# One spread of the reciprocals instead of eight, its product placed later, and rests of weights kept further from their roundings

## The chip, the core and the metric

The kernel runs on one core of a Trainium2 chip. The core has five engines that run side by side and wait for each other by semaphores: TensorE (PE, with its weight loads PEld), VectorE (DVE), ScalarE (ACT), GpSimd (POOL) and SyncE (SP). SP, POOL and ACT also issue DMAs, which sixteen DMA engines carry out. The metric is the device time of one execution in microseconds; lower is better. A profile is one execution recorded by the hardware profiler.

## The reference: what is computed

One input `x` of 2048 rows and 512 columns goes through two branches, and a gate mixes them. The attention branch has 32 heads of width 16 that share one set of keys and values. The other branch is a dense layer of width 1792 with a squared ReLU.

```python
g = _sigmoid((x * gate_w).sum(-1, keepdims=True))
# attention: 32 query heads of width 16, one key and one value head
scores = jnp.einsum("bhqd,bkd->bhqk", q, k) * (Dh ** -0.5)
p = _softmax(scores, axis=-1)
o = jnp.einsum("bhqk,bkd->bhqd", p, v)
a = o.transpose(0, 2, 1, 3).reshape(B, S, H * Dh) @ wo
# dense branch
r = jnp.where(h > 0, h, 0)          # h = x @ w1 + b1
b = (r * r) @ w2 + b2
return g * a + (1 - g) * b
```

## The kernel before

**Tiles and loops.** The 2048 queries are cut into 4 chunks of 512 (`NC`, `CH`), the 32 heads into 8 groups of 4 (`NG`). For each chunk and group the kernel walks over the 16 tiles of 128 keys and over the two halves of the chunk: 1024 steps in all. A step computes scores of 128 keys for 4 heads and 256 queries on PE, their exponentials on ACT (`e`), and then the context products on PE (`acc<-e,v_ext`). The values carry a column of ones, so that `acc` holds the sums of the exponentials beside the unnormalised outputs. Everything in single precision that needs full accuracy is split into a rounded part and a rest (`w1r` and `w1l`, for example), and each product is made from three terms.

**Phases.** The program is written out by a planner in Python at build time. It emits PE's work in phases of 6 or 7 steps: scores, mixed with the products of the dense branch, of the query projection or of the output projection ("units", L1144), by fixed patterns (`PLANS`), and behind them the context products of a phase (L825). Most scores go to PSUM tiles `s`, which ACT reads directly (L802). Some go to a single PSUM bank `x`; DVE copies them to `e` (L786, "copy"), and only then may PE write `x` again.

**What sets DVE's order.** The planner keeps estimated times of PE, ACT and DVE (`at_pe`, `at_act`, `at_dve`). Work for DVE that isn't bound to a place stands in lists: rests of weights, `divisions`, and `chores` (casts and rests of other tiles). Ahead of each copy `spend()` places as much of it as fits until that copy's scores are due. An entry of `divisions` has a duration and a time from which it may run; a rest of weights may run from the estimated end of its rounding plus `SURE`, if ACT did the rounding. None of these numbers is a wait in the program: they only decide where in DVE's queue an instruction stands. What it waits for there, semaphores decide.

**A division.** When a pair of head groups is finished (15 times in the main path), ACT copies `acc` to `accs`, SP moves the outputs to `oc` and the sums to `lq`. DVE clamps the sums and notes whether that changed them, and takes reciprocals (`n`, L854). They lie 32 to a partition, and must be repeated for the 16 rows of each head. So POOL writes `n` to HBM (`ls<-n`, L855) and reads it back spread over 128 partitions (`lc<-ls`, L857). DVE then multiplies (`oc<-oc,lc`, L864), and POOL writes the result to HBM (`oTs<-oc`, L898), from where SP loads it back into `stage` for the output projection (L1000, for the last pair L1017).

**POOL's other work.** POOL's queue is in order. It also holds the stores of the queries' rests (`qs<-ql`, L358) in the first 160 us, the fills of `res` with the bias (L697, four for each chunk), and the loads and stores of the projection (`big<-ress` L217, `out<-big` L221).

**A unit's roundings.** When a hidden unit of the dense branch is done, DVE adds the bias and clamps (L675), squares (L676), rounds (`hr`, L195) and takes the rest (L196).

Of the kernel before, what the change touches and what calls it, by code (L numbers as in the profile page):

```python
# [15 lines left out]
OP = mybir.AluOpType  # L16
# [6 lines left out]
NC, CH = 4, 512  # L23
# [9 lines left out]
ROOT = float(0x1fbd1df5 + 0x80000)  # L33
WARM = 10
LW = 4 * CH // 64
LANDS, DIVIDES, WRITES, SPREADS, SURE = 6.0, 10.0, 14.0, 8.0, 0.7
PAIR, CONTEXT, TURN, EXP, COPY, LATE = 0.235, 0.429, 0.36, 0.925, 0.66, 0.3
GROUPS = (0, 1, 2, 3), (4, 5, 6, 7), (8, 9, 10), (11, 12, 13)
AHEAD = 4
# [19 lines left out]
LAST_OK = NC * KT - 1  # L59
# [106 lines left out]
def mix_kernel(ctx: ExitStack, tc: tile.TileContext, xT, wkv, wq, wo, w12, b1, b2, cst, out):  # L166
    nc = tc.nc
# [7 lines left out]
    ls = dram.tile([NC * KT, 8, CH], F32, name="ls")  # L175
# [55 lines left out]
    with fast, tc.tile_pool(name="at", bufs=1) as at, \  # L231
# [616 lines left out]
        def divide(o, l, i, ready):  # L848

            n = at.tile([128, LW], F32, name="n")  # L850
            wide = at.tile([128, CH], F32, name="lc", bufs=2)

            def over():
                nc.vector.reciprocal(n, n)  # L854
                nc.gpsimd.dma_start(ls[i].rearrange("a (b n) -> (a b) n", b=16), n)  # L855
                for k in range(8):
                    nc.gpsimd.dma_start(wide[16 * k:16 * k + 16], bass.AP(tensor=ls.tensor, offset=ls[i, k].offset,  # L857
                                                                          ap=[[0, 16], [1, CH]]))

            return ((0.1, ready, lambda: nc.vector.tensor_scalar(n, l, L_MIN, L_MAX, op0=OP.max, op1=OP.min)),  # L860
                    (0.2, ready, lambda: nc.vector.scalar_tensor_tensor(l, n, 1.0, l, op0=OP.mult, op1=OP.is_equal,
                                                                        accum_out=ok[:, i:i + 1])),
                    (0.3, ready, over),
                    (0.72, ready + SPREADS, lambda: nc.vector.tensor_tensor(o, o, wide, OP.mult)))  # L864

        sums = []

        def finish(it, q, acc):
# [25 lines left out]
            if u == 1:  # L894
                divisions.extend(divide(o, l, 4 * c + t, at_act + (LANDS if (c, t) == (NC - 1, 2) else DIVIDES)))

                def done():
                    nc.gpsimd.dma_start(oTs[it - 1:it + 1].rearrange("u d n -> (u d) n"), o)  # L898
                    complete.add((c, t))

                divisions.append((0.0, 0.0, done))
# [443 lines left out]
```

## Time and profile before

| | us |
|---|---|
| three runs | 1226.89, 1227.65, 1228.5 (median 1227.65) |
| profiled execution | 1226.17 |
| its span | 1224.4 |
| busy: PE / ACT / DVE / POOL | 1194.5 / 1058.2 / 743.2 / 131.4 |
| DVE's 524 copies `e<-x` | 362.4, with 396.4 idle before them |
| ACT's exponentials, from PSUM / from copies | 748.5 / 278.1 |
| POOL's 120 issues of the spread `lc<-ls` | 58.2 |
| granted clock of TensorE, mean | 0.994 of full speed |

A row of the timeline gives start, length, engine, line of the program, operation, output and inputs, and in brackets the idle time of that engine before it with what ended it. Idle time of an engine matters only where another one waits for it in turn. The views of waits give the sum, the number of times and the longest.

### The profile page before, as it was taken

To read this page: it belongs to the slowest core of one execution; us is meant where nothing else is said; L and a number is where in the kernel's file an instruction comes from. 1 tells how busy PE (TensorE), PEld (TensorE's weight loads), DVE (VectorE), ACT (ScalarE), POOL (GpSimd) and SP (SyncE) were. 2 spreads that over 40 slices of the span, in tenths; PEclk is the share of its full clock that TensorE was granted. 3 is DMA by queue.
4 is the path that set the end of the run, shared out by engine and by line. 5 is a ranking of instruction groups with operands and counts; after the bars stand their busy time and mean duration, and the time that the engine had idled before them with its cause. 6 is when DMAs were issued, how large, how long until landed. Compare 5 with 4: busy or idle time off the path is not lost.

```text
span 1224.4 us, 31785 instructions
## 1 busy us (share of the span) xinstructions
PE 1194.5 (98%) x13686; PEld 788.2 (64%) x13686; DVE 743.2 (61%) x1221; ACT 1058.2 (86%) x1211; POOL 131.4 (11%) x222
## 2 busy tenths in 40 slices
PE   9999899999999999999999999999999999999997
PEld 4566566666666666665666666666666666666663
DVE  6766476666655755646647755657448655566333
ACT  6798699888999989888998988899998898889883
POOL 1001211001010110101003021100104011010100
PEclk9999899999999999999999999999999999999999
DMA  6334332121222223101313123201222222111101
GB/s 227 86 101 120 96 100 66 48 68 54 66 88 92 80 63 105 58 28 50 96 53 114 62 64 104 63 28 53 72 80 71 88 64 95 36 46 34 39 36 37
DMA packets 49338, 89.71 MB, mean 73 GB/s; under 512 B 14362, under 2 KB 14858, under 8 KB 48680
## 3 DMA queue, kind: packets, MB, share of 16 engines
q1 hardware_dynamic: 36664, 64.58, 17.0%
q0 software_dynamic: 12384, 22.77, 6.3%
q8 instruction: 109, 1.79, 0.6%
q14 instruction: 37, 0.30, 0.1%
q10 hardware_dynamic: 144, 0.26, 0.1%
HBM read 61.76 MB, written 21.22 MB: 68 GB/s over the span
## 4 chain that ended last, share of the span: by engine, by line
PE 43%; issue 42%; POOL 5%; DMA 5%; DVE 3%; ACT 1%; DVEq 0%; POOLq 0%; SPq 0%; ACTq 0%
PE acc L825 17%; PE mm L1144 14%; PE s L765 9%; POOL lc L857 3%; DMA ls<-n 3%; PE x L765 2%; DMA lc<-ls 1%; DVE e L786 1%; POOL res L697 1%; DMA xf<-in_xT 0%; POOL out L221 0%; PE mm L299 0%; DVE oc L864 0%; ACT e L802 0%; PE mm L203 0%
## 5 line engine op out<-in xcount | busy, mean ns | idle before, releaser
L802 ACT ACTIVATE e<-s 128x1024 f32<-128x1024 f32 x762 | 748.5, 1029 | 120.7 <-PE s L765 61.6
L786 DVE COPY e<-x 128x512 f32<-128x512 f32 x524 | 362.4, 692 | 396.4 <-PE x L765 308.8
L825 PE MATMUL acc<-e,v_ext 128*32 128x256 f32 (+1 forms) x8064 | 475.8, 385 | 0.0
L765 PE MATMUL s<-qa,k_aug 49*128 49x512 f32 x1524 | 440.7, 416 | 0.1
L825 PEld LDWEIGHTS acc<-e,v_ext 128*32 128x32 f32 x8064 | 246.4, 110 | 198.6 <-issue 54.7
L765 PEld LDWEIGHTS s<-qa,k_aug 49*128 49x128 f32 x1524 | 230.7, 185 | 97.0 <-ACT e L802 73.4
L802 ACT ACTIVATE e<-e 128x1024 f32<-128x1024 f32 x262 | 278.1, 1062 | 12.7 <-DVE e L786 12.6
L765 PE MATMUL x<-qa,k_aug 49*128 49x512 f32 x524 | 220.2, 420 | 19.4 <-DVE e L786 17.2
L1144 PE MATMUL mm<-w2r,hr 64*128 64x512 f32 x752 | 157.7, 393 | 0.0
L765 PEld LDWEIGHTS x<-qa,k_aug 49*128 49x128 f32 x524 | 96.6, 184 | 49.7 <-DVE e L786 27.9
L1144 PEld LDWEIGHTS mm<-w2r,hr 64*128 64x128 f32 x752 | 105.5, 187 | 12.8 <-issue 0.8
L1144 PE MATMUL mm<-w2l,hr 64*128 64x512 f32 x376 | 91.9, 392 | 0.0
L855 POOL DMA_DIRECT2D ls<-n x15 | 8.4, 562 | 587.0 <-DVE n L854 524.9
L1144 PE MATMUL mm<-xlagain,w1r 64*128 64x512 f32 x224 | 66.9, 392 | 0.0
L1144 PE MATMUL mm<-xragain,w1r 64*128 64x512 f32 x224 | 66.4, 392 | 0.0
L1144 PE MATMUL mm<-xl,w1r 64*128 64x512 f32 x224 | 65.1, 391 | 0.0
L1144 PE MATMUL mm<-xr,w1r 64*128 64x512 f32 x224 | 65.1, 392 | 0.0
L1144 PEld LDWEIGHTS mm<-w2l,hr 64*128 64x128 f32 x376 | 58.3, 186 | 6.0
L857 POOL DMA_DIRECT2D lc<-ls x120 | 58.2, 492 | 32.8 <-DMA ls<-n 32.5
L1144 PE MATMUL mm<-more 64*128 64x512 f32 x216 | 58.1, 392 | 0.0
L1144 PE MATMUL mm<-xragain,w1l 64*128 64x512 f32 x224 | 51.1, 392 | 0.0
L1144 PE MATMUL mm<-xr,w1l 64*128 64x512 f32 x224 | 50.5, 392 | 0.0
(169 smaller groups left out, 1223.8 us busy)
## 6 DMA issues: line engine op xcount, KB each, us to landing
stage<-in_w SPq DMA_DIRECT2D x56, 256.0 KB
qa<-qs SPq DMA_DIRECT2D x186, 64.0 KB
w1f<-in_w SPq DMA_DIRECT2D x28, 256.0 KB
w2f<-in_w SPq DMA_DIRECT2D x28, 256.0 KB
qs<-qr SPq DMA_DIRECT2D x16, 256.0 KB
ress<-res POOLq DMA_DIRECT2D x4, 1024.0 KB, 4.3
qs<-ql POOLq DMA_DIRECT2D x15, 256.0 KB, 7.7
oc<-accs SPq DMA_DIRECT2D x30, 128.0 KB
```

What stands on the lines that cost most here:

```text
L697: nc.gpsimd.tensor_scalar(part, b2t[0], omg[:, s:s + 1], None, op0=OP.mult)
L765: nc.tensor.matmul(dst.rearrange("p (a n) -> p a n", a=2), k_aug[rows, kt * 128:(kt + 1) * 128], qa[it][rows, :, q * HC:q * HC + HC], star ...
L786: nc.vector.tensor_copy(e_half(u)[:, 2 * r:2 * r + 2], x.rearrange("p (a n) -> p a n", a=2))
L802: nc.scalar.activation(e_half(u), src, AF.Exp, scale=SCALE)
L825: nc.tensor.matmul(accs[q][h * 32:(h + 1) * 32], v_ext[:, kt], es[u // 2][:, h % 2 * 2 + h // 2, u % 2 * HC:u % 2 * HC + HC * n], start=(k ...
L855: nc.gpsimd.dma_start(ls[i].rearrange("a (b n) -> (a b) n", b=16), n)
L857: nc.gpsimd.dma_start(wide[16 * k:16 * k + 16], bass.AP(tensor=ls.tensor, offset=ls[i, k].offset, ap=[[0, 16], [1, CH]]))
L1144: nc.tensor.matmul((self.before if r else self).bank, a[p], b[p], start=not r and i == 0, stop=r == 1 and i == len(self.terms[1]) - 1, ski ...
```

## The change

`SPREADS`, the planner's distance from the estimated time of the reciprocals to the product, goes from 8 to 14, for the last division of the main path to 10. `SURE`, its distance from the end of a rounding on ACT to the rest of the same weights, goes from 0.7 to 1.4. The eight transfers that spread the reciprocals, each one row of 512 numbers repeated into 16 partitions, become one of eight rows, each repeated 16 times, into 128 partitions. Lines behind L857 have a number one lower in the changed kernel.

```diff
-LANDS, DIVIDES, WRITES, SPREADS, SURE = 6.0, 10.0, 14.0, 8.0, 0.7
+LANDS, DIVIDES, WRITES, SPREADS, SURE = 6.0, 10.0, 14.0, 14.0, 1.4
...
             def over():
                 nc.vector.reciprocal(n, n)
                 nc.gpsimd.dma_start(ls[i].rearrange("a (b n) -> (a b) n", b=16), n)
-                for k in range(8):
-                    nc.gpsimd.dma_start(wide[16 * k:16 * k + 16], bass.AP(tensor=ls.tensor, offset=ls[i, k].offset,
-                                                                          ap=[[0, 16], [1, CH]]))
+                nc.gpsimd.dma_start(wide, bass.AP(tensor=ls.tensor, offset=ls[i].offset,
+                                                  ap=[[CH, 8], [0, 16], [1, CH]]))
...
-                    (0.72, ready + SPREADS, lambda: nc.vector.tensor_tensor(o, o, wide, OP.mult)))
+                    (0.72, ready + (SPREADS if i < LAST_OK - 1 else LANDS + 4.0), lambda: nc.vector.tensor_tensor(o, o, wide, OP.mult)))
```

Since the numbers steer the planner, instructions move along the whole program. Two places show it.

DVE in the third division, from the reciprocals to the unit behind it, before:

```order
L854 RECIPROCAL n<-n 128x32
L786 COPY e<-x 128x2x256 x2
L700 SCALAR_TENSOR_TENSOR res_2278<-mm,omg,res_2278 128x512
L786 COPY e<-x 128x2x256 x2
L864 TENSOR_TENSOR oc<-oc,lc 128x512
L786 COPY e<-x 128x2x256 x2
L700 SCALAR_TENSOR_TENSOR res_2278<-mm,omg,res_2278 128x512
L786 COPY e<-x 128x2x256
L495 TENSOR_TENSOR w2l<-w2f,w2r 128x512
L786 COPY e<-x 128x2x256 x3
L675 TENSOR_SCALAR big<-mm,b1t 128x512
```

and in the changed kernel:

```order
L854 RECIPROCAL n<-n 128x32
L786 COPY e<-x 128x2x256 x2
L700 SCALAR_TENSOR_TENSOR res_2271<-mm,omg,res_2271 128x512
L786 COPY e<-x 128x2x256 x4
L700 SCALAR_TENSOR_TENSOR res_2271<-mm,omg,res_2271 128x512
L786 COPY e<-x 128x2x256
L863 TENSOR_TENSOR oc<-oc,lc 128x512
L786 COPY e<-x 128x2x256
L495 TENSOR_TENSOR w2l<-w2f,w2r 128x512
L786 COPY e<-x 128x2x256 x2
L675 TENSOR_SCALAR big<-mm,b1t 128x512
```

The product stands behind seven copies instead of four, and the rest `w2l` behind one copy more of its phase.

POOL in the fifth division, from the write of the reciprocals to the projection's first loads, before:

```order
L855 DMA ls<-n 128x32
L857 DMA lc<-ls 16x512 x8
L697 TENSOR_SCALAR res_5247<-big,omg 128x512
L898 DMA oTs<-oc 128x512
L697 TENSOR_SCALAR res_5247<-big,omg 128x512 x2
L217 DMA big<-ress 128x512 x2
```

and in the changed kernel:

```order
L855 DMA ls<-n 128x32
L856 DMA lc<-ls 128x1x512
L697 TENSOR_SCALAR res_5219<-big,omg 128x512 x2
L897 DMA oTs<-oc 128x512
L697 TENSOR_SCALAR res_5219<-big,omg 128x512
L217 DMA big<-ress 128x512 x2
```

Eight issues become one, and two of the fills of `res` stand between the spread and `oTs`, where one stood.

## The prediction

> **What bounds the kernel now.** I read the page first, then the chain that ended last in order of time, then busy time by stretches, then the waits, and last the timeline around one division.
>
> ```profile
> span 1224.4 us, 31785 instructions
> PE 1194.5 (98%) x13686; PEld 788.2 (64%) x13686; DVE 743.2 (61%) x1221; ACT 1058.2 (86%) x1211; POOL 131.4 (11%) x222
> ```
>
> PE is busy 98% of the span, so it looks as if only less work on PE could help. The ends of matmuls are modelled, though, so I look for PE's rhythm instead: where each block of context products (`acc`) starts.
>
> ```profile
> 286.65 3.16 PE acc L825 x56
> ...
> 294.42 3.16 PE acc L825 x56
> 302.22 3.16 PE acc L825 x56
> ...
> 951.36 3.16 PE acc L825 x56
> ...
> 1160.65 2.73 PE acc L825 x48
> 1167.34 2.73 PE acc L825 x48
> ```
>
> I call the time from one `acc` block to the next a phase. A phase of 56 context products takes 7.80 us (294.42 to 302.22), one of 48 takes 6.69 (1160.65 to 1167.34). The phases are so regular that whatever lengthens one can be read off directly. I cut out the phases in which DVE's product `oc*lc` of a division stands, with the phase behind the seventh: 16 stretches for 15 divisions, bounded by the starts of `acc`. Shown are the first, the last, those used below, and the sum over all 16 (columns: stretch, its length, PE's busy time and instructions, granted clock, DMA share, GB/s).
>
> ```profile
> 128.85:143.85 15.00, 10.79 (x97) 0.77 0.38 99
> ...
> 278.03:286.58 8.55, 8.02 (x96) 1.00 0.13 35
> ...
> 421.87:430.83 8.96, 7.25 (x73) 1.00 0.25 61
> ...
> 564.46:575.67 11.21, 8.48 (x95) 0.97 0.18 50
> 575.67:584.78 9.11, 9.11 (x96) 0.85 0.18 59
> ...
> 713.62:720.28 6.66, 6.66 (x73) 1.00 0.20 41
> ...
> 932.49:941.54 9.05, 8.07 (x96) 1.00 0.46 119
> ...
> 1147.23:1153.90 6.67, 6.67 (x80) 1.00 0.13 34
> sum 142.71, PE 127.05; mean PE 7.94
> ```
>
> Eleven of the 16 are phases of 56, three are phases of 48, and two are shorter ones with 32 context products; of these I take the one at 713.62 (6.66 us) as undisturbed. Without a disturbance they would take 11 x 7.80 + 3 x 6.69 + 2 x 6.66 = 119.2 us. They take 142.71: **23.5 us are lost there**, 7.2 of them in the first. The phases behind are 7.77 and 7.80 long (286.65, 294.42, 302.22), so nothing of a loss is caught up later. The clock column (0.77 in the first, 0.85 behind the seventh) shows that the loss holds a slower TensorE too.
>
> What causes it:
>
> ```profile
> DVE oc L864 <- DMA lc<-ls: 25.9, 13, 6.5
> ...
> PE x L765 <- DVE e L786: 17.2, 14, 3.7
> ```
>
> Thirteen times DVE stands still for `lc`, 25.9 us in all. In one division, from the timeline:
>
> ```profile
> 276.38 0.35 DVE L854 RECIPROCAL n<-n 128x32 f32<-128x32 f32 x1
> ...
> 277.05 0.55 POOL L855 DMA_DIRECT2D ls<-n  x1 [62.15 <-DVE n L854]
> ...
> 279.02 3.85 POOL L857 DMA_DIRECT2D lc<-ls  x8 [1.42 <-DMA ls<-n]
> ...
> 284.81 0.69 DVE L864 TENSOR_TENSOR oc<-oc,lc 128x512 f32<-128x512 f32 x1 [1.01 <-DMA lc<-ls]
> ...
> 286.16 0.49 PE L765 MATMUL x<-qa,k_aug 49*128 49x512 f32 x1 [0.53 <-DVE e L786]
> ```
>
> The reciprocals start at 276.38, the spread is issued from 279.02 (2.64 later) to 282.87, and the product starts at 284.81. Behind it on DVE is a copy of scores out of the single bank `x`, and PE's next scores for that bank wait for the copy.
>
> **The change part by part.**
>
> *One spread for eight.* POOL issues for 3.85 us now; the rows of single 128-partition transfers on POOL are 0.54 to 0.70. How long the new transfer takes to land is not in the trace. The nearest row is the load of `big`, 256 KB from HBM into 128 partitions on the same queue; the far end is the write of `ql`, 256 KB too, but split 4x32:
>
> ```profile
> L217 POOL DMA_DIRECT2D big<-ress x12: 536/543/611, 432.7 to 1017.0; - x12
> ...
> DMA to landing us min/median/max: 2.9/3.3/4.7
> ```
> ```profile
> L358 POOL DMA_DIRECT2D qs<-ql x15: 688/697/896, 38.2 to 155.4; - x15
> ...
> DMA to landing us min/median/max: 6.4/7.7/9.6
> ```
>
> I take 3.3; the ends are 2.9 and 9.6. `lc` is then whole 2.64 + 3.3 = 5.9 us after the reciprocals start, at worst 12.2.
>
> The Trainium skill, "DMA: Bandwidth & Descriptors", section "Why a DMA increments its semaphore by 16 and not by 1", speaks against this part: a transfer runs on the largest number of engines, up to 16, that divides the slowest dimension of both sides. By it the new spread (8x16 rows into 128 partitions) has 8 engines where each old one had 16, and its sum would put some 0.9 us on the landing and nothing on the time. The slow rows of `ql` (slowest dimension 4) agree with it.
>
> *The product further behind.* By the order it stands 4 to 9 copies of scores behind the reciprocals, before 2 to 4. The shortest distance that I find is in the fifth division, where it comes behind the sixth copy, the addition into `res` and a rounding:
>
> ```profile
> 419.47 0.35 DVE L854 RECIPROCAL n<-n 128x32 f32<-128x32 f32 x1
> ...
> 423.65 0.43 DVE L195 CAST hr<-big 128x512 fp32r<-128x512 f32 x1
> ...
> 430.87 0.69 DVE L786 COPY e<-x 128x512 f32<-128x512 f32 x1 [0.59 <-PE x L765]
> 431.48 0.74 DVE L700 SCALAR_TENSOR_TENSOR res<-mm,omg,res 128x512 f32<-128x512 f32 x1
> ```
>
> 431.48 + 0.74 + some 0.4 for the rounding, less the 2.23 that DVE waits there today, is 430.4: 10.9 us after the reciprocals. Elsewhere it is 11.3 to 15.7 by the same count. Against 5.9 that leaves 5 us; against the far end of 12.2 a few divisions would wait up to 1.3 us each, little beside today's 25.9. So the waits go, and with them **-23.5 us**. What is late next at those places is nothing that I find: a product of 0.69 then stands between two copies like a rest of weights, and phases with a rest take 7.80.
>
> The first division is special: its `ls` lands late, behind a write of `ql`.
>
> ```profile
> 129.15 3.87 POOL L857 DMA_DIRECT2D lc<-ls  x8 [7.57 <-DMA ls<-n]
> ```
>
> `lc` would be whole at 132.5 (with 3.3) to 138.8 (with 9.6); the product's place, three copies and one unit's roundings later, comes at some 134.6. I put **+0.5** (0 to 4) back.
>
> What is queued behind the product moves with it: POOL's write `oTs` (in the first division now behind a write of `ql`, in the fifth behind one more addition for `res`, in the ninth behind one load of `big`), and SP's reload of it, which the order also puts later, behind the stores of `accs`. No engine waits for these. The projection of the third chunk misses its turn and stands 9 phases later; the number of products in each phase stays the same up to the last eight phases, so PE has no gap there: 0.
>
> *The rests of weights.* Most of the 112 move one copy later, in the same phase. DVE's groups, first and last of five:
>
> ```profile
> L495 DVE TENSOR_TENSOR w1l<-w1f,w1r 128x512 fp32r<-128x512 f32 x28 | 19.1, 683 | 0.0
> ...
> L495 DVE TENSOR_TENSOR more<-stage,more 128x512 fp32r<-128x512 f32 x9 | 6.1, 681 | 0.0
> ```
>
> No rest waits for its rounding today (idle 0.0), so nothing can be gained. Lost could be PE time if a copy comes late; today rests stand behind the first, second or third copy of a phase, and phases of all three kinds take 7.8 us. I take 0; the ends are 0 and 11 (0.1 us for each).
>
> *POOL against DVE.* While POOL fills `res`, DVE's work from SBUF to SBUF runs longer:
>
> ```profile
> 941.38 6.35 POOL L697 TENSOR_SCALAR res<-big,omg 128x512 f32<-128x512 f32 x4
> ...
> 944.19 2.12 DVE L195 CAST hr<-big 128x512 fp32r<-128x512 f32 x1
> ...
> 948.05 0.50 PE L765 MATMUL x<-qa,k_aug 49*128 49x512 f32 x1 [1.69 <-DVE e L786]
> ```
>
> The cast takes 2.12 us for 0.43, PE waits 1.69, and this phase (941.54 to 951.3) is 1.95 too long. POOL is free 3.3 us earlier now, so in the fifth division two of these fills start at about 422.7 (419.47 + 2.64 + 0.6) and last some 3.2, under the unit's cast at 423.65: +1.7. In the twelfth one moves ahead of `oTs` and three are left behind the product: of the 1.95 I take 0.7 off. Together **+1.0** (-2 to +6).
>
> *The end.* The last division's product comes some 5 us later, and by the order six product instructions (three pairs over two row halves) go from two late phases into the two last ones with scores.
>
> ```profile
> 1179.04 0.70 PE mm L1144 x6
> ```
>
> Six cost 0.70; the phases that lose them give some back: **+0.3** (0 to 0.7).
>
> Sum: -23.5 + 0.5 + 1.0 + 0.3 = -21.7. The profiled execution took 1226.17 us (its span and 1.8 around it), so 1204.5. That execution lies 1.48 below the median of the three runs shown (1227.65), which themselves spread 1.6; I add 1.0 and predict **1205.5 us**.
>
> **The rivals.**
>
> *Part is given back by POOL (A).* Four groups of fills are free to move, and a collision costs up to 1.95. Three more give 5.9: 1211.4. For it: the fifth division, where the order puts two fills right behind the spread. Against: only one of the groups costs much today.
>
> *The rests break the rhythm (B).* 11 us for the 112: 1216.5. Against it stand the phases of 7.8 with rests at every place.
>
> *The spread runs on very few engines (C, slower).* Its rows are read from one leading dimension of 8 with repeats.
>
> ```profile
> q0 software_dynamic: 12384, 22.77, 6.3%
> ```
>
> 6.3% of 16 engines for 1224.4 us is 1234 us for 22.77 MB, so one engine moves 18.5 KB a us and would take 14.2 us for 262 KB. With 1.5 of start `lc` is whole 18.3 after the reciprocals; places at 13.5 on average leave 4.8 x 15 = 72 us of DVE waiting. Today 25.9 of it cost 23.5, so 72 would cost 65: about 1270. It decides from the point where `lc` comes some 15.2 us after the reciprocals, which leaves the waits of today, 1.7 a division. For it: the writes of `ql` show that a shape can double a landing. Against: even these stay under 9.7, among much more traffic.
>
> *PE was not the bound (D, no change).* If ACT (86%) set the phases, they would stay long, about 1226. Against it: neighbours of the long phases take 7.80 with the same exponentials.
>
> **How the numbers follow.** The likeliest case (1202 to 1209) has 0.70; A 0.14, B 0.05, C 0.06, D 0.03; 0.02 is for less than 1202 (no collision at all, a free end). The range 1201.5 to 1212 holds the likeliest and A, 0.84. A measurement of this kernel tells about 0.2% (2.5 us) from no change: faster 0.91 (likeliest, A, B and the low end), same 0.03 (D), slower 0.06 (C).
>
> **What would show it.** In the profile after, DVE's wait for `lc` is under 2 us in all and the wait of PE's `x` for copies under 6. `lc` is issued 15 times, 0.5 to 0.7 us each, and lands in 3 to 4.5. The phases of the 15 products take 7.8 or 6.7, the first under 9, with the clock at 1.00 there. The fifth division's unit shows a cast of over 1 us. The prediction is wrong if `lc` lands later than 10 us, if DVE waits for it anyway, or if phases without a product have grown.

## The result, and the profile after

The changed kernel took **1212.51 us** (median; 1207.87 to 1217.13), against 1227.66 before in the same series (1226.89 to 1228.5). The ratio is 0.9876, with a 95% interval of 0.9838 to 0.9915: faster by 1.2%. The forecast of 1205.5 was 7 us too low, and the top of its range, 1212, lies half a microsecond under the median.

The profiled execution took 1212.43 us with a span of 1210.7. The head of its page:

```profile
span 1210.7 us, 31619 instructions
PE 1190.7 (98%) x13685; PEld 789.5 (65%) x13686; DVE 744.7 (62%) x1222; ACT 1056.5 (87%) x1209; POOL 84.4 (7%) x117
```

The span is 13.7 shorter; the forecast, in the same terms, was 21.7. POOL lost 47 us of work, 105 instructions fewer. That this by itself moved the time isn't seen: a run below that keeps POOL's old work takes 1212.7. First the waits on `lc` and on the copies of scores, and the issue and landing of the spread (from the waits of DVE and PE, and the view of the tile `lc`):

```profile
DVE oc L863 <- DMA lc<-ls: 3.6, 1, 3.6
```
```profile
PE x L765 <- DVE e L786: 6.8, 4, 3.1
```
```profile
L856 POOL DMA_DIRECT2D lc<-ls x15: 613/623/635, 130.4 to 1130.4; - x15
...
DMA to landing us min/median/max: 3.4/3.7/7.5
```

DVE waits for `lc` once where it waited thirteen times, 3.6 us for 25.9. PE's waits for copies fell from 17.2 to 6.8. The transfer usually lands 3.7 after its issue, near the 3.3 taken; one took 7.5.

Now the stretches that hold the products, cut out in the same way as before. Again the stretch behind one of them is taken in, here that of the first (columns: stretch, its length, PE's busy time and instructions, PEld, DVE, ACT, POOL, granted clock, DMA share, GB/s):

```profile
128.50:139.86 11.36, 8.23 (x100) 5.62 (x98) 5.35 (x9) 7.88 (x9) 2.08 (x4) 1.00 0.40 120
139.86:149.31 9.45, 9.45 (x98) 5.93 (x97) 4.56 (x7) 5.80 (x6) 1.27 (x2) 0.82 0.43 89
211.42:219.19 7.77, 7.77 (x99) 5.25 (x102) 4.02 (x6) 6.57 (x7) 0.62 (x1) 1.00 0.28 85
...
428.24:436.04 7.80, 7.80 (x100) 5.38 (x102) 5.55 (x9) 6.94 (x8) 3.26 (x4) 1.00 0.28 96
...
1139.46:1146.14 6.68, 6.68 (x80) 4.40 (x78) 2.96 (x6) 5.81 (x7) 0.57 (x1) 1.00 0.12 42
sum 127.10, PE 123.97 PEld 82.89 DVE 77.25 ACT 108.89 POOL 17.26; mean PE 7.75 PEld 5.18 DVE 4.83 ACT 6.81 POOL 1.08
```

Thirteen of these 16 are phases of 56 context products and three of 48: undisturbed 13 x 7.80 + 3 x 6.69 = 121.5. They take 127.1. So 5.6 us are lost where 23.5 were, and 5.2 of them in the first division's two stretches (11.36 + 9.45 - 15.6). The other fourteen products cost 0.4 together.

What is left of the forecast's gain went to three places. The first division, on the queues of POOL, SP and DVE:

```profile
119.71 0.70 POOL L358 DMA_DIRECT2D qs<-ql  x1 [6.93 <-DVE n L859]
120.61 0.59 POOL L855 DMA_DIRECT2D ls<-n  x1 [0.21 <-issue]
130.36 0.64 POOL L856 DMA_DIRECT2D lc<-ls  x1 [9.16 <-DMA ls<-n]
131.00 0.70 POOL L358 DMA_DIRECT2D qs<-ql  x1
```
```profile
129.86 0.56 SPq L358 DMA_DIRECT2D qs<-qr  x1
130.51 0.60 SPq L475 DMA_DIRECT2D w1f<-in_w  x1
```
```profile
137.89 0.69 DVE L863 TENSOR_TENSOR oc<-oc,lc 128x512 f32<-128x512 f32 x1 [3.65 <-DMA lc<-ls]
```

Two stores of the queries (`qs<-qr`, `qs<-ql`) and a load of weights are issued within 0.7 us of the spread. It lands 7.5 after its issue, and the product waits 3.65. In the kernel before, no store by SP came near the spread, whose eight issues began at 129.15, for the rounding of `qr` stood behind the waiting product on DVE:

```profile
122.27 0.56 SPq L358 DMA_DIRECT2D qs<-qr  x1
...
136.76 0.56 SPq L358 DMA_DIRECT2D qs<-qr  x1
```
```profile
134.84 0.69 DVE L864 TENSOR_TENSOR oc<-oc,lc 128x512 f32<-128x512 f32 x1 [6.54 <-DMA lc<-ls]
...
136.06 0.68 DVE L395 CAST qr<-mm 128x512 fp32r<-128x512 f32 x1
```

In the changed kernel that rounding stands ahead of the product:

```profile
129.15 0.68 DVE L395 CAST qr<-mm 128x512 fp32r<-128x512 f32 x1
```

The fifth division, in the stretch ahead of its product, on DVE, POOL and PE:

```profile
418.76 0.75 DVE L676 TENSOR_TENSOR big<-big 128x512 f32<-128x512 f32 x1
419.55 2.11 DVE L195 CAST hr<-big 128x512 fp32r<-128x512 f32 x1
421.69 1.05 DVE L196 TENSOR_TENSOR hr<-big,hr 128x512 fp32r<-128x512 f32 x1
422.67 0.68 DVE L786 COPY e<-x 128x512 f32<-128x512 f32 x1
```
```profile
418.80 4.28 POOL L697 TENSOR_SCALAR res<-big,omg 128x512 f32<-128x512 f32 x2
```
```profile
423.40 0.53 PE L765 MATMUL x<-qa,k_aug 49*128 49x512 f32 x1 [2.19 <-DVE e L786]
```

Two fills of `res` lie exactly on a unit's rounding and rest, as the forecast said they might. The cast takes 2.11 instead of 0.43 and the rest 1.05 instead of 0.69, the copy behind them comes late, and PE waits 2.19. What that costs, and what a second such place costs in the eighth division, the stretches show:

```profile
417.73:428.24 10.51, 8.32 (x75) 5.58 (x78) 7.83 (x10) 6.65 (x9) 4.90 (x3) 0.84 0.09 27
647.41:656.72 9.31, 8.07 (x96) 5.32 (x94) 7.86 (x9) 7.35 (x9) 6.90 (x5) 1.00 0.32 111
```

The first, with 32 context products, takes 6.66 undisturbed: 3.85 lost, more than PE's wait of 2.19, since the granted clock is only 0.84 there. The second loses 1.51 at full clock.

The third place is the end, where the phase from the one late block of `acc` to the next grew from 5.20 to 5.97 (before, then after):

```profile
1199.70:1204.90 5.20, 5.20 (x55) 3.34 (x54) 1.42 (x4) 5.10 (x7) 0.00 (x0) 1.00 0.02 5
```
```profile
1185.31:1191.28 5.97, 5.46 (x56) 3.31 (x54) 1.39 (x3) 5.13 (x7) 0.00 (x0) 1.00 0.02 4
```

### The profile page after: what moved, and what is told of

It is laid out like the page before. It is cut to its first block, busy times and chain, and to the rows that moved or that the text cites. A ratio compares the mean times of both kernels' runs of the same rounds, so it can differ in the third digit from the quotient of the medians.

```text
span 1210.7 us, 31619 instructions
## 1 busy us (share of the span) xinstructions
PE 1190.7 (98%) x13685; PEld 789.5 (65%) x13686; DVE 744.7 (62%) x1222; ACT 1056.5 (87%) x1209; POOL 84.4 (7%) x117
## 4 chain that ended last, share of the span: by engine, by line
PE 86%; issue 9%; DVE 2%; DMA 1%; POOL 1%; ACT 0%; SPq 0%; POOLq 0%
PE acc L825 34%; PE mm L1143 29%; PE s L765 17%; PE x L765 4%; POOL qs L358 1%; DMA lc<-ls 1%; DVE e L786 1%; DVE hr L195 0%; DMA xf<-in_xT 0%; PE mm L203 0%; DVE hr L196 0%; PE mm L299 0%; DVE big L676 0%; DVE big L675 0%; PE s L966 0%
## 5 line engine op out<-in xcount | busy, mean ns | idle before, releaser
L765 PEld LDWEIGHTS x<-qa,k_aug 49*128 49x128 f32 x524 | 96.5, 184 | 36.4 <-DVE e L786 13.8
L700 DVE SCALAR_TENSOR_TENSOR res<-mm,omg,res 128x512 f32<-128x512 f32 x64 | 47.5, 741 | 0.0
```

The costliest lines, as they stand in the source:

```text
L700: nc.vector.scalar_tensor_tensor(part, p, omg[:, s:s + 1], part, op0=OP.mult, op1=OP.add)
L765: nc.tensor.matmul(dst.rearrange("p (a n) -> p a n", a=2), k_aug[rows, kt * 128:(kt + 1) * 128], qa[it][rows, :, q * HC:q * HC + HC], star ...
```

## The experiments

**The changed kernel again.** Nothing is edited; the question is whether the first division's stall belongs to the order or to the run.

> The changed kernel once more, for a second profile and for the spread of its runs. Theory 1: the first division's spread lands late because the stores of a query unit and a load of weights are issued beside it, and this landing varies from run to run; the phases of the first division are then again 3 to 8 us too long in all, by another amount than in the first profile (5.2), and the median is 1210 to 1214 with a spread of several us. Theory 2 (rival): the first division's loss is fixed by the order and repeats within 0.5 us; then the spread of the runs comes from elsewhere.

It took 1209.91 (1207.28 to 1216.83, six runs), ratio 0.986 (0.9829 to 0.989). With the first four, ten runs of the same kernel have a median of 1211.0 and lie within 9.9 us. In this profile no product waits at all, and the first division's stretches are undisturbed:

```profile
129.10:137.04 7.94, 7.94 (x100) 5.50 (x101) 5.36 (x9) 7.15 (x9) 1.34 (x2) 1.00 0.51 134
137.04:144.90 7.86, 7.86 (x99) 5.33 (x102) 4.57 (x8) 6.44 (x7) 2.01 (x3) 1.00 0.47 117
...
1169.80:1208.30 38.50, 28.03 (x260) 15.79 (x259) 12.21 (x30) 13.68 (x16) 0.00 (x0) 0.86 0.08 30
```

There the longest landing of the spread is 4.7, not 7.5. The same two stores and the same load stand beside it, but `ls` landed 1.7 earlier, and so SP's store came behind the spread:

```profile
129.22 0.64 POOL L856 DMA_DIRECT2D lc<-ls  x1 [7.45 <-DMA ls<-n]
```
```profile
130.48 0.56 SPq L358 DMA_DIRECT2D qs<-qr  x1
```

1.26 behind it here, 0.50 ahead of it in the first profile. That the order of these two decides the landing is my reading of two profiles, not a trial. Profiles of versions below bear it out only in part. With the store 0.49 and 0.22 ahead the spread landed in 7.5 and 6.5 (both edits with the old rests, and the first product later), and with the store 0.57 and 1.16 behind in 4.6 and 4.3 (the old rests, and both edits); but with the fills on DVE it landed in 6.8, though the store came 2.1 behind. That the stall varies from one execution to another is shown, against the rival. The 3 to 8 us of theory 1 are not there either: the two stretches lose 0.2, and the median lies just under its range. Yet this span is 1208.3, only 2.4 shorter: the end behind the last phases takes 38.50 at a clock of 0.86, where the other profile has 36.30 at 0.93. The runs spread from more than one place.

**The first product later.**

```diff
-(0.72, ready + (SPREADS if i < LAST_OK - 1 else LANDS + 4.0), lambda: nc.vector.tensor_tensor(o, o, wide, OP.mult)))
+(0.72, ready + (SPREADS + 8.0 * (i == 0) if i < LAST_OK - 1 else LANDS + 4.0), lambda: nc.vector.tensor_tensor(o, o, wide, OP.mult)))
```

> The first division's product alone is put 8 us further behind (11 copies behind its reciprocals instead of 7). Theory 1 (the late spread of the first division costs 5.2 us and most of the spread between runs): DVE's wait of 3.6 us is gone, the phases there take 7.8 each, the median is 1206 to 1208, and the runs lie within 3 us. Rival (the loss there is TensorE's slower clock or the stores themselves, not the wait): the phases stay long and the median stays at 1211 to 1213.

1209.69 (1208.78 to 1215.22), ratio 0.9857 (0.9831 to 0.9884). DVE's wait for `lc` was gone, as theory 1 said, but the gain expected from it wasn't there, and the runs still spread 6 us. The profile names a new place in the first chunk:

```profile
159.40:171.46 12.06, 9.48 (x96) 6.11 (x94) 7.73 (x12) 7.65 (x10) 3.24 (x3) 0.89 0.43 132
```
```profile
168.33 1.11 DVE L495 TENSOR_TENSOR w1l<-w1f,w1r 128x512 fp32r<-128x512 f32 x1
169.36 0.68 DVE L786 COPY e<-x 128x512 f32<-128x512 f32 x1
169.96 1.04 DVE L619 TENSOR_TENSOR wol<-stage,wor 128x512 fp32r<-128x512 f32 x1
```

In this stretch 4.3 us are lost. PE waits 2.58 at 168.46 for a copy that stands behind a cast, which had waited 3.55 for the load of `wo`; then two rests run beside POOL's fills, 1.11 and 1.04 for 0.68 and 0.69. Whether the edit brought this about isn't settled. The wait for `wo` stands in two later profiles too (2.99 and 2.62), one of them without this edit, and in another that has the edit it is 1.09.

**The fills of `res` on DVE.** POOL keeps its DMAs; its sixteen multiplications go to DVE, with their duration told to the planner.

```diff
-nc.gpsimd.tensor_scalar(part, b2t[0], omg[:, s:s + 1], None, op0=OP.mult)
+dve(0.46); nc.vector.tensor_scalar(part, b2t[0], omg[:, s:s + 1], None, op0=OP.mult)
```

> The changed kernel with the sixteen fills of the res tiles on DVE instead of POOL. Theory 1 (POOL's fills hold up DVE's roundings, 3.9 us in the fifth division and 1.5 in the eighth): no rounding of a unit lasts 1 us or more, these phases take 6.6 and 7.8, and the median is 5 to 6 us below the changed kernel's, 1206 to 1208. Rival (DVE's sixteen added instructions, 0.43 us each, cost as much in other phases): the median stays within 1.5 us of the changed kernel's.

1204.37 (1202.08 to 1213.07), ratio 0.9823 (0.9791 to 0.9855): 5.5 us below the repeat of the changed kernel in the same series. DVE's groups of roundings and fills (count, busy time, mean ns, idle before), of the changed kernel and of this one:

```profile
L195 DVE CAST hr<-big 128x512 fp32r<-128x512 f32 x47 | 23.8, 506 | 1.6
```
```profile
L195 DVE CAST hr<-big 128x512 fp32r<-128x512 f32 x47 | 20.1, 427 | 1.6
...
L697 DVE TENSOR_SCALAR res<-big,omg 128x512 f32<-128x512 f32 x16 | 7.7, 479 | 0.0
```

The mean cast falls from 506 to 427 ns: none is slowed any more. DVE has 7.7 us more to do, and these runs show no cost of it. On POOL the same sixteen took 1.55 to 2.22 us each. Theory 1 said this difference of 5 to 6; its time, 1206 to 1208, was 2 too high. Not all of it is part of the miss, for fills cost time in the kernel before too.

**Both edits.** The fills on DVE, and the first product later.

> Both of these edits. Theory 1: the two losses add up, 5.2 and 5.4 us, so the median is 1201 to 1203.5, with runs that lie within 3 us of each other. Rival (one loss hides part of the other, or a third wait takes over): 1204 or more.

1202.88 (1201.04 to 1207.21), ratio 0.9805 (0.9779 to 0.9831). The profile's span is 1199.6; all product phases have their undisturbed length, and the spread's longest landing is 4.3. The time lies in theory 1's range, but not as a sum of two losses: the later product alone had gained 0.2, and against that version (1209.69) the removal of the fills from POOL gains 6.8. The runs spread 6 us, not 3.

**The one transfer alone.** The kernel before with only this edit:

```diff
-for k in range(8):
-    nc.gpsimd.dma_start(wide[16 * k:16 * k + 16], bass.AP(tensor=ls.tensor, offset=ls[i, k].offset,
-                                                          ap=[[0, 16], [1, CH]]))
+nc.gpsimd.dma_start(wide, bass.AP(tensor=ls.tensor, offset=ls[i].offset,
+                                  ap=[[CH, 8], [0, 16], [1, CH]]))
```

> The kernel before with the one transfer alone: the products stay at their old places, 2 to 4 copies of scores behind the reciprocals. Theory 1 (either part alone is enough): the spread is whole 2.6 + 3.7 = 6.3 us after the reciprocals, DVE reaches most products about 7.4 us after them, so its wait for the spread falls from 25.9 to under 5 us (left: the fourth and fifth division, which have only 2 and 3 copies between), and the time is 1208 to 1214. Theory 2 (both parts are needed): the places are too near for any landing that varies by 2 us; DVE still waits over 10 us, and the time is 1217 or more.

1214.23 (1209.43 to 1217.68), ratio 0.9889 (0.9839 to 0.9939). DVE's wait for `lc`, and the stretch of the first division:

```profile
DVE oc L863 <- DMA lc<-ls: 7.5, 2, 7.3
```
```profile
128.80:145.40 16.60, 11.33 (x97) 7.40 (x96) 5.17 (x8) 7.67 (x10) 2.64 (x4) 0.79 0.40 111
```

Apart from the first division, DVE waits 0.2 us for `lc`. That division alone waits 7.3 and takes 16.6 where 7.8 would do. Theory 1 held in the main. The wait left over is 7.5, where under 5 was said, it stands in the first division and not in the fourth and fifth, and the time is 0.2 above the range.

**The later places alone.** Eight transfers and the old rests, with the new distances of the product.

```diff
-LANDS, DIVIDES, WRITES, SPREADS, SURE = 6.0, 10.0, 14.0, 8.0, 0.7
+LANDS, DIVIDES, WRITES, SPREADS, SURE = 6.0, 10.0, 14.0, 14.0, 0.7
...
-(0.72, ready + SPREADS, lambda: nc.vector.tensor_tensor(o, o, wide, OP.mult)))
+(0.72, ready + (SPREADS if i < LAST_OK - 1 else LANDS + 4.0), lambda: nc.vector.tensor_tensor(o, o, wide, OP.mult)))
```

> The kernel before with the later places alone: eight transfers as before, products 4 to 9 copies behind the reciprocals, rests of weights where they were. Theory 1 (either part alone is enough): the eight small transfers are whole some 9 us after the reciprocals, the places stand 10.9 us or more behind them, so DVE's wait falls from 25.9 to under 4 us and the time is 1206 to 1214; the issues of 3.85 us keep POOL's fills of res back, so that fewer of them may lie on DVE's roundings than with one transfer. Theory 2 (both parts are needed): DVE still waits over 10 us and the time is 1217 or more.

1212.7 (1212.58 to 1213.0), ratio 0.9875 (0.9837 to 0.9913). Only the first product waits, 4.7 us where under 4 was said, and its phase and the next lose 7.7; fourteen are free, and POOL's busy time is still 131.8. So either part alone takes away most of the waits, and the two together gain little more than one, if anything: their gains don't add. Fills lie on roundings in the phases at 646.8 and 939.3 and cost 1.85 and 1.29 here; in the fifth division they start at 424.73, behind the cast, which keeps its 0.43, and the stretch loses 0.4. Which fills collide depends on when POOL comes free.

**The rests of weights alone.**

```diff
-LANDS, DIVIDES, WRITES, SPREADS, SURE = 6.0, 10.0, 14.0, 8.0, 0.7
+LANDS, DIVIDES, WRITES, SPREADS, SURE = 6.0, 10.0, 14.0, 8.0, 1.4
```

> The kernel before with the larger distance of the rests of weights alone (1.4 for 0.7). No rest waits for its rounding before, so my theory (the term of 0) says 1226 to 1229, DVE's wait for the spread 24 to 28 us, and phases of 56 context products without a division as long as before (7.80). The rival (the rests break the rhythm, 0.1 us for each of 112) says 1231 or more; if the rests were what gained, it would be under 1222.

1231.87 (1226.93 to 1242.6, ten runs), ratio 1.0044 (1.0014 to 1.0075): slower by 0.44%, some 5 us. The time lies in the rival's range, not in mine, but not by the rival's mechanism: phases without a product are as long as before (7.80). What grew is the wait for the spread:

```profile
DVE oc L864 <- DMA lc<-ls: 32.4, 13, 7.8
```
```profile
207.60:218.40 10.80, 8.05 (x96) 5.42 (x94) 4.03 (x6) 7.92 (x9) 6.67 (x11) 1.00 0.19 52
218.40:227.90 9.50, 9.50 (x96) 6.11 (x94) 3.42 (x5) 5.81 (x6) 0.03 (x1) 0.82 0.22 72
```

25.9 became 32.4. In the second division the shifted rests put a copy ahead of the reciprocals that stood behind them: the product comes behind three copies, not four, and waits 3.25 us, not 1.49. The phase loses 3.0, and the next one another 1.7 at a clock of 0.82. In the twelfth the places are as before, but `ls` took longer to land (POOL waits 3.02 for 1.44) and the product waits 4.50, not 1.49. Behind these waits the ninth division's phases lose 3.8 us and the twelfth's 8.0, at clocks of 0.85 and 0.78. Other divisions lose less than before: the seventh's two phases take 7.96 and 8.86 for 11.21 and 9.11, and the thirteenth's 7.78 for 10.34. For these I have only the one profile, and how much belongs to the order and how much to the run stays open.

**Sixteen rows for eight.** The reciprocals are written twice, so that the spread reads 16 rows, each repeated 8 times.

```diff
-nc.gpsimd.dma_start(ls[i].rearrange("a (b n) -> (a b) n", b=16), n)
+for k in range(2):
+    nc.gpsimd.dma_start(bass.AP(tensor=ls.tensor, offset=ls[i, k].offset,
+                                ap=[[2 * CH, 8], [LW, 16], [1, LW]]), n)
 nc.gpsimd.dma_start(wide, bass.AP(tensor=ls.tensor, offset=ls[i].offset,
-                                  ap=[[CH, 8], [0, 16], [1, CH]]))
+                                  ap=[[CH, 16], [0, 8], [1, CH]]))
```

> The changed kernel with the reciprocals written twice into HBM, so that the spread reads 16 rows, each repeated 8 times, where it read 8 rows, each repeated 16 times; one more small write for each division. If the number of rows sets the number of DMA engines, the landing falls from 3.7 to about 2.8 us, DVE's wait in the first division gets 1 to 3 us shorter, and the time stays within 3 us of the changed kernel (1208 to 1213), since the other products don't wait. If the spread already runs on all sixteen engines, the landing stays at 3.4 to 3.9. Over 1215 would mean that the second write on POOL's queue costs more than it gives.

1213.28 (1210.03 to 1217.57), ratio 0.9886 (0.9839 to 0.9933): no change that the runs can tell, as expected where fourteen of the fifteen products wait for nothing. The first still waits, and against the expectation for longer, 4.3 us for 3.6: the second write is issued only at 129.06, and so the spread at 134.13, not at 130.36.

```profile
DVE oc L865 <- DMA lc<-ls: 4.3, 1, 4.3
```
```profile
DMA to landing us min/median/max: 2.9/3.2/5.1
```

The median landing falls from 3.7 to 3.2, where 2.8 was expected. Stretches of 5 us around the spread of the third division, with hardly any other transfer on the DMA engines, show what changed (40 slices of 0.125 us, the busy share of the sixteen engines in tenths; the changed kernel first, then this one):

```profile
DMA  0000000000007633345545331610000000000000
```
```profile
DMA  0000000000009945956520400000000000000000
```

With eight rows the share is mostly 3 to 5 tenths behind its first two slices, with sixteen up to 9, and the bulk is through in about 1.4 us for 1.9. So the number of rows sets how much of the sixteen engines the transfer keeps busy at once (the view doesn't count engines), and what it saves is the half microsecond of moving, not the start and the end of a landing. The Trainium skill's rule that the prediction weighed ("DMA: Bandwidth & Descriptors", section "Why a DMA increments its semaphore by 16 and not by 1") agrees with these shares; the 0.9 us that I had worked out by it was too much.

**The old rests in the changed kernel, and in the version with both edits.** `SURE` goes back to 0.7 in each.

```diff
-LANDS, DIVIDES, WRITES, SPREADS, SURE = 6.0, 10.0, 14.0, 14.0, 1.4
+LANDS, DIVIDES, WRITES, SPREADS, SURE = 6.0, 10.0, 14.0, 14.0, 0.7
```

> The changed kernel with the rests of weights as before (0.7 for 1.4): one transfer and later places stay. Theory 1 (the rests cost nothing by themselves; the 4 us that they cost alone in the kernel before came from the waits for the spread, which the shifted order made longer): with the waits gone the time is that of the changed kernel, 1208 to 1214, and the phases without a product are as long as there. Theory 2 (the rests cost by themselves): 1205 to 1208, and the phases of 56 context products that hold rests are shorter.

1208.92 (1207.28 to 1212.34), ratio 0.9828 (0.9776 to 0.9881).

> The version with the fills on DVE and the first product later still, with the rests of weights as before (0.7 for 1.4). Theory 1 (the rests cost nothing by themselves): 1201 to 1205, within 1.5 us of that version's 1202.9. Theory 2 (the rests cost by themselves): under 1200.

1201.95 (1201.74 to 1204.76), ratio 0.9762 (0.9713 to 0.9811). Both lie in theory 1's ranges, 2.1 and 0.9 below their partners, which is within the spread of the runs. The partners ran in other series, though, and by the ratios to the kernel before the distances are 4 to 6 us, with intervals that overlap, so the times alone don't decide. The phases do. From the block of context products at 172.24 to the one at 413.28 the changed kernel takes 241.04, and with the old rests the same phases, from 167.46 to 408.69, take 241.23; from the fifth division's product to the eighth's both take 211.25. Over these stretches, more than a third of the span, the rests cost nothing once the products don't wait.

**The first division on another queue.** The write of the reciprocals and its spread go through SP for the first division.

```diff
-nc.gpsimd.dma_start(ls[i].rearrange("a (b n) -> (a b) n", b=16), n)
-nc.gpsimd.dma_start(wide, bass.AP(tensor=ls.tensor, offset=ls[i].offset,
+via = nc.sync if i == 0 else nc.gpsimd
+via.dma_start(ls[i].rearrange("a (b n) -> (a b) n", b=16), n)
+via.dma_start(wide, bass.AP(tensor=ls.tensor, offset=ls[i].offset,
```

> The changed kernel, where in the first division alone the write of the reciprocals and its spread go through SP's queue, not through POOL's behind the store of ql. Theory 1 (the write waits in its queue behind the 256 KB store): ls lands 1.7 to 3.5 us after its issue where it took 9.5, lc is whole by 130, DVE's wait for it (3.6 us in the changed kernel's profile) is gone, phases of the first division 7.8 each, median 1207 to 1210 with runs within 5 us; the fills' cost of 5 us stays. Rival (the sixteen engines themselves are full in that stage): ls still takes 6 us or more on the other queue, the wait stays, and the time with it, 1210 to 1213 with runs 8 us apart.

1208.41 (1207.23 to 1213.56), ratio 0.9835 (0.9779 to 0.989). The highest of the four is the profiled one, whose first context product starts at 41.8 us, not at 36.0: a late start has nothing to do with divisions. The other three lie between 1207.23 and 1209.18. No product waits. But the reason given for it fell:

```profile
SPq L857 <- DMA ls<-n: 5.4, 1, 5.4
```

The write of 16 KB still takes over 5 us behind SP's own stores of `nrm`, away from the 256 KB store on POOL's queue. The rival's claim, that the transfers of that stage are in each other's way on any queue, fits that better, though 5.4 is less than the 6 it named, and the write stood behind other stores here too. Its forecast of the time failed, since 5.4 is short enough for the place where the product stands. Theory 1's time came true, for another reason than its own.

**All that the runs pointed to.** Fills on DVE, the first division through SP, old rests.

> All that the runs point to in one: the fills of res on DVE, the first division's write and spread through SP's queue, the rests of weights at the old distance of 0.7; product places as in the changed kernel. If the three act by themselves, 1200 to 1203, no product waits, and runs within 4 us. If moving the first division off POOL's queue holds back SP's loads of weights by its wait of some 5 us, 1204 or more with new gaps of PE between 120 and 160 us.

1203.68 (1203.04 to 1206.68), ratio 0.9798 (0.9743 to 0.9853). No product waits, and in the first chunk two phases, at 159.7 and 169.6, take 9.89 and 9.45: PE waits 1.86 there for a copy, at a lower clock behind it. The time is 0.7 above the first forecast and 0.3 below the second, which had named gaps between 120 and 160 us. Nothing is won over the versions with the first product later. Those, 1202.88 and 1201.95, beat both kernels, and each lies 7.0 us below the version with POOL's fills in its own series (1209.91 and 1208.92); between the two the runs don't decide.

## Why the prediction was wrong, step by step

The steps against the two profiles (spans 1224.4 and 1210.7):

| step | predicted | found |
|---|---|---|
| waits for the spread | -23.5 | 0.4 left outside the first division: -23.1 |
| put back in the first division | +0.5 (0 to 4) | +5.2 in this profile, 0.2 in the repeat |
| rests of weights | 0 (0 to 11) | none to be seen in phases without a product |
| POOL's fills against DVE | +1.0 (-2 to +6) | +3.0 |
| the end | +0.3 (0 to 0.7) | +0.8 |
| sum | -21.7 | -14.1; the spans differ by 13.7 |

POOL's row is 3.85 in the fifth division and 1.51 in the eighth, less the 1.95 and 0.39 that the same kind of collision cost in the kernel before. The sum goes 0.4 further than the spans, and the first context product, which starts 0.4 earlier than before (36.0 for 36.4), widens that to 0.8. Phases that lengthened without a cause that I can name, one by 0.33 (at 989.2), one by 0.17 (at 1050.8) and many by less than 0.1, close the table to within a few tenths.

**What held.** The main term did: PE's rhythm is the bound, a product that doesn't wait costs nothing, and fourteen of fifteen products stand in phases within 0.3 us of the undisturbed length. The landing was 3.7 for 3.3. `lc` was issued 15 times at 0.61 to 0.64. POOL's relief brought nothing that the runs tell. No queue behind the product mattered: POOL's write of `oTs` now stands waiting for DVE 132.1 us in all, and no engine waits for it. The rivals C (few engines) and D (PE not the bound) are out. So is B: the rests don't break the rhythm of phases without a product. Alone, in the kernel before, they do cost some 5 us, but the one profile shows that as longer waits for the spread, which the other parts take away. Of the signs that the prediction named, the issues of `lc` and the slow cast came. DVE's wait (3.6, not under 2), PE's wait for copies (6.8, not under 6), the longest landing (7.5, not 4.5) and the first division's phase (11.36, not under 9) did not come as forecast.

**What failed: two terms of the sum were mis-sized.** The first is the first division. The range of its landing (3.3 to 9.6) held the 7.5 found, and the place of the product was right too (134.2 reached, 134.6 forecast). But the chosen value of +0.5 rested on an early landing, while the stage is full of transfers. What I hadn't seen is that DVE's stall was itself holding back SP's store and load: once the product stands behind them, they run beside the spread. And a wait of 3.65, of which PE feels 3.12, costs 5.2, for the phase behind it runs at a clock of 0.82. The step also has no single value: of the same kernel's two profiles one loses 5.2 and the other 0.2. In the medians it doesn't show: with this wait gone the kernel took 1209.69, beside 1209.91 for the repeat. What made the spread land late stays open; the stores beside it are only part of an answer.

The second is the fills. The forecast named the fifth division, the two fills and the cast; it took 1.7 for them. They met the cast and the rest behind it in full, PE waited 2.19, and the clock fell to 0.84: 3.85. That fall isn't fixed either: in two other profiles the same stretch with the same wait ran at full clock and took 9.03 and 8.98. The eighth division I hadn't counted as a place at all, though a collision cost 0.39 there before. Of the 7.6 us by which the table's two sums differ, the first division has 4.7 and the fills 2.0; the end and the other products have the last 0.9. Rival A, at 1211.4, comes nearest to the time, but in part by luck: the largest part in this profile is the first division, which A doesn't have. That the fills cost 5 us or more in all is shown by their removal (1204.37 against 1209.91, and 1202.88 against 1209.69 with the first product later), and 2.3 of it was in the kernel before already.

What stays open is the spread of the runs, some 10 us for the changed kernel. Five places of it are seen in profiles (the start, the first division, the load of `wo` near 165, the clock in the fifth division, the end), but no run here says what sets them.

## What to carry to other kernels

Where two parts of a change remove the same wait, the sum gets its worth once: either part alone was worth 13 to 15 us here, and both together 15 to 18. Work that a stall holds back comes free with it, so before a stall is written off, list what waits for the stalled engine and which transfers and engines it will meet. And a rhythm like PE's is best costed by its undisturbed phases: the loss of a stall is its length and, at times, a slow phase behind it.

## What the runs showed of the hardware

A stall of PE can cost more than its length, and the same stall doesn't always. In the fifth division PE waits 2.2 us for the same late copy in five profiles. Three of them ran that stretch at a granted clock of 0.84 and took 10.49 to 10.56 (waits of 2.19, 2.26 and 2.19: the changed kernel, its repeat, the first division on another queue). Two ran it at 1.00 and took 9.03 and 8.98 (2.25 and 2.21: the first product later, and the old rests):

```profile
417.32:426.35 9.03, 6.78 (x72) 4.62 (x71) 7.94 (x10) 6.26 (x9) 4.90 (x3) 1.00 0.11 31
```
```profile
413.08:422.06 8.98, 6.76 (x72) 4.39 (x70) 7.56 (x9) 6.26 (x9) 4.91 (x3) 1.00 0.09 31
```

So the length of a wait doesn't decide it alone. Over all profiles, PE's waits for a copy of 1.69 us or less that stood by themselves left the clock at 1.00, and those of 2.58 or more lowered it, there or in the stretch behind. Between these, 1.86 lowered it once and 2.31 in the kernel before didn't. Short waits close together can do it too: 0.47, 0.17 and 0.61 within 2.5 us, in the run with the rests alone, brought that phase to 0.85. After waits of 2.19 and 3.12 the changed kernel lost 1.7 more each. The Trainium skill, "TensorE: Matmul & The Clock Gate", section "Part 1: The HAM clock gate", has the clock set by how busy PE was in free-running windows of about 3.4 us. That different outcomes follow the same wait agrees with windows that run free; that waits of 1.86 to 2.3, less than such a window, can be enough is this case's number beside it.

POOL's multiplications from SBUF to SBUF and DVE's work there slow each other: the cast goes from 0.43 to 2.11 us, the subtraction of two SBUF tiles from 0.69 to 1.05 (once to 1.44), and POOL's own from 1.55 to as much as 2.22. A copy from PSUM beside them keeps its 0.68. On DVE the same multiplication takes 0.48, less than the time that it costs DVE when POOL does it under a cast.

One and the same 256 KB spread landed in 3.4 to 7.5 us within one execution, and a 16 KB write in 1.7 to 9.5; the longest of both stand in the first division, among stores and loads.
